# A seven-tap convolution and a gated layer on Trainium2: how the tap weights reach the 128 partitions

## The chip, the core and the metric

The kernel runs on one core of a Trainium2 chip. Five engines with queues of their own work side by side: TensorE (PE: matmuls, and PEld for its weight loads), VectorE (DVE), ScalarE (ACT), GpSimd (POOL) and SyncE (SP). SP, ACT and POOL also issue DMA transfers between the main memory (HBM) and the on-chip memory of 128 partitions. Matmuls write to PSUM, an accumulator of 128 partitions, and VectorE or ScalarE take the results out of it. The engines wait for each other, and for transfers, with semaphores[...].

The metric is device time in microseconds (us), median of several runs. The kernel before took 690.42 us (three runs, 689.95 to 690.78). Profiles are of one run each, and their span leaves out a little at the ends: 688.2 us for the kernel before.

## The reference, cut to what matters

```python
# x: 8 x 4096 x 192, weight: 8 heads x 7 taps, w_in: 192 x 2048, w_out: 2048 x 192, beta: 2048
w = softmax(weight, axis=-1)                 # exp(weight - max) / (sum + 1e-9), per head
x_pad = concat([zeros(8, 6, 192), x], axis=1)
conv[b, s, 24*h + g] = sum over k of w[h, k] * x_pad[b, s + k, 24*h + g]
h = conv.reshape(32768, 192) @ w_in
g = h * sigmoid(beta * h)                    # swish with a beta for each of the 2048 columns
out = g @ w_out
```

Channel 24h+g belongs to head h. Only the seven taps of each head, 56 numbers in all, come from `weight`; before they can be used they must stand in each partition that holds a channel of that head.

## The kernel before

The rows are cut into two streams (NS = 2) that run in the two halves of the partitions. The 192 channels are stored as 64 groups of three (Q = 64, NK = 3), so 64 partitions hold one stream and eight neighbouring partitions share a head. A step is a stretch of rows of both streams; steps 0, 1 and 2 are small (128, 128 and 256 rows), so that the pipeline fills quickly. From step 3 on VectorE computes the convolution. For the first 512 rows TensorE does: the taps, times an identity matrix, are its weights (`diag`), and 14 matmuls per 128 rows add up the seven shifted products of the two streams.

The loads that the start needs. The taps come as two transfers that repeat each head's row for its eight partitions, one for each half, after the first block of x on the same two queues:

```python
taps = consts.tile([128, K], FP32, name="taps")
for s, eng in enumerate((nc.sync, nc.scalar)):
    pin(eng.dma_start(out=x0[:, 0, s, :], in_=xs[s, 0:128, :]))
for s, eng in enumerate((nc.sync, nc.scalar)):
    pin(eng.dma_start(out=taps[half_of(s), :],
                      in_=weight[:, None, :].to_broadcast([H, Q // H, K])))
# ... beta16 and x0 of block 1 follow on nc.sync
# nc.scalar then loads its table for Exp
# GpSimd: ident = affine_select(...), then it issues the loads of w_in (256, 384 and 384
# columns for each half), xb0 (blocks 2 and 3 of x), w_out, ...
```

The softmax numerators, the weights of the convolution, and the first block. `warm` issues matmuls on a constant whose results nobody reads:

```python
warm(9, 256)                                       # 9 matmuls of 256 columns
cv0 = psum_h.tile([128, 2, TILE], FP32, name="ph")
pin(nc.vector.tensor_reduce(out=nmax, in_=taps, axis=AX.X, op=ALU.max, negate=True))
pin(nc.scalar.activation(etap, taps, AF.Exp, bias=nmax, accum_out=tsum))
for k in range(2):
    make_diag(k)                                   # VectorE: diag[k] = ident2 * etap[:, k]
# ...
t = transpose_0(pa[0], x0, 0)                      # TensorE: 3 transposes of 128x128 f32
take_0(t, 0, act=True)                             # ScalarE: xr <- PSUM
warm(6, 128)
for k in range(2, K):
    make_diag(k)
# ...
pin(nc.scalar.activation(scrap, one, AF.Silu))     # brings the table of Silu in early
b0 = [cv0[:, 0, :], pb[0]]
conv_0(b0, 0)                                      # 7 taps x 2 streams = 14 matmuls of 384 columns
evac_0(b0, 0, 0, nc.scalar)
evac_0(b0, 0, 1, nc.vector)                        # xcp, the input of step 0
t1 = transpose_0(pa[1], x0, 1)
pin(nc.tensor.transpose(beta_ps, beta16, ident[0:NF, 0:NF]))
```

Step 0 then runs u = 0 to 7. Each u has six matmuls with `w_in` into one PSUM tile `ph` (of which there are two) and two activations of 128x256 on ScalarE (`gp`); between them TensorE transposes and convolves the next blocks:

```python
def first_tile(i, u):
    if (i, u) == (0, 1):
        take_0(transpose_0(pa[0], xb0, 0), 2)      # needs xb0, block 2
        conv_0(pb, 1, 0, 1)
    elif (i, u) == (0, 2):
        take_0(transpose_0(pa[1], xb0, 1), 3)      # needs xb0, block 3
        conv_0(pb, 1, 1, 2)
    # ... further taps and blocks
```

u = 5 is the first to use the last 384 columns of `w_in`.

Of the kernel before, what the change touches and what calls it, by code (L numbers as in the profile page):

```python
# [10 lines left out]
FP32 = mybir.dt.float32  # L11
FP32R = mybir.dt.float32r
BF16 = mybir.dt.bfloat16
AF = mybir.ActivationFunctionType
ALU = mybir.AluOpType
AX = mybir.AxisListType
# [3 lines left out]
def kernel(  # L20
# [9 lines left out]
    nc = tc.nc  # L30

    B, S, D = x.shape
    H, K = weight.shape
# [5 lines left out]
    Q = D // NK  # L39
    NS = 2  # L40
# [5 lines left out]
    def pin(ins):  # L46

        return tc.keep_in_program_order(ins)
# [4 lines left out]
    consts = ctx.enter_context(tc.tile_pool(name="consts", bufs=1))  # L53
# [55 lines left out]
    def half_of(s):  # L109
        return slice(64 * s, 64 * s + 64)  # L110
# [8 lines left out]
    x0 = consts.tile([128, 2, NS, D], FP32, name="x0")  # L119
    xb0 = consts.tile([128, 2, NS, D], BF16, name="xb0")  # L120
    xb1 = consts.tile([128, 2, NS, D], BF16, name="xb1")
    taps = consts.tile([128, K], FP32, name="taps")
    for s, eng in enumerate((nc.sync, nc.scalar)):
        pin(eng.dma_start(out=x0[:, 0, s, :], in_=xs[s, 0:128, :]))  # L124
    for s, eng in enumerate((nc.sync, nc.scalar)):
        pin(eng.dma_start(out=taps[half_of(s), :],
                          in_=weight[:, None, :].to_broadcast([H, Q // H, K])))
    beta16 = consts.tile([NF, 128], FP32, name="beta16")
    pin(nc.sync.dma_start(out=beta16, in_=moe_beta.rearrange("(c p) -> c p", p=128)))
    HF = F // 2  # L130
# [1 line left out]
    def load_x0(b, eng):  # L132
# [7 lines left out]
    scrap = consts.tile([128, 1], FP32, name="scrap")  # L140
    pin(nc.scalar.activation(scrap, one, AF.Exp))

    ident = consts.tile([128, 128], FP32, name="ident")
    pin(nc.vector.memset(ident, 0.0))
    pin(nc.gpsimd.affine_select(out=ident, in_=ident, compare_op=ALU.not_equal, fill=1.0,
                                base=0, pattern=[[-1, 128]], channel_multiplier=1))
    for f0, f1 in ((0, 256), (256, 640), (640, HF)):
# [7 lines left out]
    for s in range(NS):  # L155
        pin(nc.gpsimd.dma_start(out=xb1[:, :, s, :],
                                in_=xs[s, TILE:TILE + 256, :].rearrange("(b p) d -> p b d", p=128)))
# [21 lines left out]
    def warm(n, cols):  # L179
        for _ in range(n):  # L180
            pin(nc.tensor.matmul(idle[:, 0, 0:cols], ones[:, 0:128], ones[:, 0:cols], start=True, stop=True))

    warm(9, 256)
    cv0 = psum_h.tile([128, 2, TILE], FP32, name="ph")
    nmax = consts.tile([128, 1], FP32, name="nmax")
    pin(nc.vector.tensor_reduce(out=nmax, in_=taps, axis=AX.X, op=ALU.max, negate=True))
    etap = consts.tile([128, K], FP32, name="etap")
    tsum = consts.tile([128, 1], FP32, name="tsum")
    pin(nc.scalar.activation(etap, taps, AF.Exp, bias=nmax, accum_out=tsum))  # L189
    diag = consts.tile([128, K, NS, Q], FP32R, name="diag")  # L190

    def make_diag(k):
# [19 lines left out]
    def take_0(t, b, act=False):  # L212
        dst = xr[:, :, PAD + 128 * b:PAD + 128 * b + 128]
        if act:
            pin(nc.scalar.activation(dst, t, AF.Copy))  # L215
        else:
            pin(nc.vector.tensor_copy(dst, t))
# [20 lines left out]
    pb = po_banks()  # L238
    t = transpose_0(pa[0], x0, 0)
    take_0(t, 0, act=True)  # L240
    warm(6, 128)
    for k in range(2, K):
        make_diag(k)
    rsum = consts.tile([128, 1], FP32, name="rsum")
# [219 lines left out]
    for i in range(NP, n_steps):  # L464
        j = steps[i][0] // TILE + 1
# [140 lines left out]
```

## Time and profile before

| What | Value |
|---|---|
| Time, median of three | 690.42 us |
| Span of the profile | 688.2 us |
| TensorE busy | 681.2 us (99%) |
| ScalarE busy | 586.5 us (85%) |
| VectorE busy | 553.2 us (80%) |
| GpSimd busy | 14.1 us (2%) |
| Share of the chain that ended last: PE, ACT, DMA | 97%, 1%, 1% |

Busy time is an average over the whole span, and TensorE is busy nearly throughout. The page's second part cuts the span into 40 slices of about 17 us; the first slice has a 7 for PE where the others have a 9. The change touches only what lies in the first 8 us, so the views to read are those with a window on the start: the chain of waits (what released what, followed back from the end), the timeline of each engine, and the list of DMA issues with the time from issue to landing. In the chain and the timeline the first column is the start in us, the second the duration of the merged group, and a bracket gives the idle time ahead of it with what ended it. The column PEclk reads full speed in the whole span, so that the pace of TensorE has to be taken from the starts of its matmuls.

### The profile page before, as it was taken

The numbers are of one execution on the slowest core, as the hardware profiler recorded it, in microseconds if no ns is written. First come the engines' busy times: TensorE is split into PE (matmuls) and PEld (weight loads), VectorE is DVE, ScalarE is ACT, GpSimd is POOL, SyncE is SP. The second block draws the span as 40 slices with busy tenths as digits, with TensorE's granted clock in tenths as the row PEclk, the third lists the DMA queues.
The fourth block names the chain that finished last, engine by engine and source line by source line (L and its number), as shares of the span: only waits on it lengthen the run. The fifth ranks groups of instructions, "written<-read, shape, count | busy, mean of one in ns | idle before, by whom it ended". The sixth has DMA issues, their size and how long they took to land.

```text
span 688.2 us, 27039 instructions
## 1 busy us (share of the span) xinstructions
PE 681.2 (99%) x12426; PEld 451.1 (66%) x12426; DVE 553.2 (80%) x902; ACT 586.5 (85%) x600; POOL 14.1 (2%) x25
## 2 busy tenths in 40 slices
PE   7999999999999999999999999999999999999998
PEld 5799986555555555555555555555555567777777
DVE  4999999999998889878889888888888898875112
ACT  5999999888888888888888888888888888888881
POOL 7000000000000000000000000000000000000000
PEclk9999999999999999999999999999999999999999
DMA  9554333354334344323344323444224443220113
GB/s 212 157 139 113 89 105 90 89 134 108 102 76 106 105 118 117 80 62 106 105 117 116 79 63 106 105 117 116 72 70 105 106 117 71 56 55 12 48 49 92
DMA packets 148977, 66.84 MB, mean 97 GB/s; under 512 B 110672, under 2 KB 148256, under 8 KB 148864
## 3 DMA queue, kind: packets, MB, share of 16 engines
q1 hardware_dynamic: 145480, 61.08, 34.5%
q0 software_dynamic: 3168, 3.93, 2.7%
q8 instruction: 97, 1.59, 1.0%
q14 instruction: 16, 0.13, 0.1%
q10 hardware_dynamic: 216, 0.10, 0.0%
HBM read 28.32 MB, written 25.17 MB: 78 GB/s over the span
## 4 chain that ended last, share of the span: by engine, by line
PE 97%; ACT 1%; DMA 1%; DVE 0%; issue 0%; SPq 0%; DVEq 0%
PE ph L330 47%; PE po L408 41%; PE po L362 6%; PE po L446 2%; PE ph L313 1%; ACT gp L317 1%; DMA taps<-in_weight_dram 1%; ACT g L317 1%; PE ph L223 0%; PE po L209 0%; PE po L223 0%; ACT etap L189 0%; SPq L124 0%; ACT xr L215 0%; DVE o_sp L368 0%
## 5 line engine op out<-in xcount | busy, mean ns | idle before, releaser
L334 ACT ACTIVATE g<-ph,beta 128x1024 bf16<-128x1024 f32 (+1 forms) x544 | 560.4, 1038 | 79.0 <-PE ph L330 63.4
L330 PE MATMUL ph<-xc,w_in_s 64*64 64x512 bf16 (+2 forms) x5856 | 589.3, 366 | 0.3 <-ACT g L317 0.3
L408 PE MATMUL po<-g,w_out_q 64*64 64x512 bf16 x5184 | 528.5, 376 | 0.0
L330 PEld LDWEIGHTS <-w_in_s 64*64 64x64 bf16 (+1 forms) x5856 | 271.5, 104 | 126.8 <-issue 0.5
L296 DVE SCALAR_TENSOR_TENSOR acc<-xt,tapn,acc 128x512 f32<-128x512 bf16 (+1 forms) x450 | 311.3, 763 | 0.9
L408 PEld LDWEIGHTS <-w_out_q 64*64 64x64 bf16 x5184 | 240.0, 105 | 91.9
L425 DVE STREAM_TRANSPOSE o_sb<-po 128x512 f32<-128x512 f32 x81 | 72.0, 889 | 110.3 <-PE po L408 110.3
L296 DVE SCALAR_TENSOR_TENSOR xc<-xt,tapn,acc 128x512 bf16<-128x512 bf16 (+1 forms) x90 | 64.1, 763 | 0.1
L362 PE MATMUL po<-w_out_s,g 64*128 64x192 bf16 x896 | 57.1, 243 | 0.0
L86 DVE CAST xb<-xf 128x768 bf16<-128x768 f32 (+1 forms) x62 | 48.7, 824 | 0.0
L362 PEld LDWEIGHTS <-g 64*128 64x128 bf16 x896 | 43.4, 94 | 3.3
L294 DVE TENSOR_SCALAR acc<-xt,tapn 128x512 f32<-128x512 bf16 (+1 forms) x90 | 41.0, 488 | 1.1
L368 DVE COPY o_sp<-po 128x192 f32<-128x192 f32 x40 | 12.7, 350 | 9.7 <-PE po L446 7.3
L313 PE MATMUL ph<-xcp,w_in_s 64*128 64x256 bf16 (+1 forms) x144 | 15.0, 316 | 0.2 <-ACT gp L317 0.2
L317 ACT ACTIVATE gp<-ph,beta 128x256 bf16<-128x256 f32 x32 | 12.4, 479 | 1.8 <-PE ph L313 1.8
L446 PEld LDWEIGHTS <-g 128*128 128x128 bf16 x128 | 10.5, 98 | 0.4 <-issue 0.4
L446 PE MATMUL po<-w_out_s,g 128*128 128x192 bf16 x128 | 10.7, 246 | 0.0
L317 ACT ACTIVATE g<-ph,beta 128x512 bf16<-128x512 f32 x16 | 9.6, 692 | 0.2
L313 PEld LDWEIGHTS <-w_in_s 64*128 64x128 bf16 x144 | 6.8, 97 | 3.6 <-issue 1.0
L223 PE MATMUL po<-xr,diag 64*128 64x384 f32 x49 | 8.9, 401 | 0.0
L362 PE MATMUL po<-w_out_s,gp 64*128 64x192 bf16 x128 | 7.2, 243 | 0.0
L362 PEld LDWEIGHTS <-gp 64*128 64x128 bf16 x128 | 5.8, 94 | 1.6
(49 smaller groups left out, 60.1 us busy)
## 6 DMA issues: line engine op xcount, KB each, us to landing
xf<-in_x_dram SPq DMA_DIRECT2D x60, 384.0 KB, 3.9
out_dram<-o_sb SPq DMA_DIRECT2D x108, 192.0 KB, 4.6
out_dram<-o_sp SPq DMA_DIRECT2D x16, 192.0 KB, 4.1
xt<-xb SPq DMA_TRANSPOSE x122, 3.0
w_out_f<-in_moe_w_out_dram POOLq DMA_DIRECT2D x4, 384.0 KB, 7.3
w_in_s<-w_in_s POOLq DMA_DIRECT2D x4, 192.0 KB, 6.0
out_dram<-o_sp SPq DMA_DIRECT2D x8, 96.0 KB, 1.6
w_in_s<-in_moe_w_in_dram POOLq DMA_DIRECT2D x4, 144.0 KB, 4.9
```

The lines of the kernel that those rows point to most:

```text
L86: pin((eng or nc.vector).tensor_copy(xbf_of[j][:, b0:b1, :, s, :].rearrange("p b k q -> p k b q"), xf_of[j][:, b0:b1, s, :].rearrange("p b ...
L294: pin(nc.vector.tensor_scalar_mul(a, src, w))
L296: pin(nc.vector.scalar_tensor_tensor(out=xc_of[i][:, k0:k1, 0:n] if k == K - 1 else a, in0=src, scalar=w, in1=a, op0=ALU.mult, op1=ALU.add))
L313: pin(nc.tensor.matmul(ph[:, h, 0:NS * n], w_in_s[half_of(h), kk, ts(fcs[h], 128)], xc_of[i][half_of(h), :, kk, :], start=(kk == 0), stop= ...
L317: pin(nc.scalar.activation(g_at(i, fcs[h])[:, :, 0:n], ph[:, h, 0:NS * n].rearrange("p (s t) -> p s t", s=NS), AF.Silu, scale=beta[:, fcs[ ...
L330: pin(nc.tensor.matmul(ph[m0:m1, s, 0:n], w_in_s[half_of(s), kk, 128 * fc + m0:128 * fc + m1], xc_of[i][half_of(s), kk, 0:n], start=(kk == ...
L334: pin(nc.scalar.activation(g_at(i, fc)[:, :, 0:n], ph[:, :, 0:n], AF.Silu, scale=beta[:, fc:fc + 1]))
L362: pin(nc.tensor.matmul(po[q][:, 0:D], g_at(i, fc)[r, s, ts(b, 128)], w_out_s[r, fc, :], start=(phase == 0 and fc == 0), stop=(phase == 1 a ...
L368: pin(nc.vector.tensor_copy(dst, po[:, 0:D]))
L408: pin(nc.tensor.matmul(po_of[i, m][half_of(s), 0:n], w_out_q[half_of(r), fc, m, :], g_at(i, fc)[half_of(r), s, 0:n], start=(first and fc = ...
L425: pin(nc.vector.transpose(osb_of[i][:, 0:n // L, :, m], po_of[i, m][:, 0:n].rearrange("p (b l) -> p b l", l=L)))
L446: pin(nc.tensor.matmul(po[:, 0:D], g_at(i, fc)[:, s, ts(b, 128)], w_out_s[:, fc, :], start=(fc == 0), stop=(fc == NF - 1)))
```

## The change

The taps are loaded once, as a tile of 8 heads by 7 taps (224 bytes), by the first transfer on SyncE's queue; SyncE's half of the first block of x follows it. A matmul spreads them: its weights are a selection matrix `sel` of 8 x 128 with a one where partition and head belong together, so its result, in an unused bank of `cv0`, holds each head's taps in each of its partitions. VectorE and ScalarE read the taps from there. VectorE clears `sel`, and GpSimd fills it ahead of `ident`. Three short filler matmuls stand between that matmul and the transposes of x, and the fillers after the transposes are seven instead of six: they give TensorE work while it would wait. The two repeating loads of the taps are gone from both queues.

```diff
-    taps = consts.tile([128, K], FP32, name="taps")
+    taps = consts.tile([H, K], FP32, name="taps")
+    pin(nc.sync.dma_start(out=taps, in_=weight))
     for s, eng in enumerate((nc.sync, nc.scalar)):
         pin(eng.dma_start(out=x0[:, 0, s, :], in_=xs[s, 0:128, :]))
-    for s, eng in enumerate((nc.sync, nc.scalar)):
-        pin(eng.dma_start(out=taps[half_of(s), :],
-                          in_=weight[:, None, :].to_broadcast([H, Q // H, K])))
...
+    sel = consts.tile([H, NS, H, Q // H], FP32, name="sel")
+    pin(nc.vector.memset(sel, 0.0))
     ident = consts.tile([128, 128], FP32, name="ident")
     pin(nc.vector.memset(ident, 0.0))
+    pin(nc.gpsimd.affine_select(out=sel, in_=sel, compare_op=ALU.not_equal, fill=1.0, base=0,
+                                pattern=[[0, NS], [-1, H], [0, Q // H]], channel_multiplier=1))
     pin(nc.gpsimd.affine_select(out=ident, in_=ident, compare_op=ALU.not_equal, fill=1.0,
                                 base=0, pattern=[[-1, 128]], channel_multiplier=1))
...
     warm(9, 256)
     cv0 = psum_h.tile([128, 2, TILE], FP32, name="ph")
     nmax = consts.tile([128, 1], FP32, name="nmax")
-    pin(nc.vector.tensor_reduce(out=nmax, in_=taps, axis=AX.X, op=ALU.max, negate=True))
+    tap_ps = cv0[:, 1, 0:K]
+    pin(nc.tensor.matmul(tap_ps, sel.rearrange("h s g j -> h (s g j)"), taps, start=True, stop=True))
+    warm(3, 128)
+    pin(nc.vector.tensor_reduce(out=nmax, in_=tap_ps, axis=AX.X, op=ALU.max, negate=True))
...
-    pin(nc.scalar.activation(etap, taps, AF.Exp, bias=nmax, accum_out=tsum))
+    pin(nc.scalar.activation(etap, tap_ps, AF.Exp, bias=nmax, accum_out=tsum))
...
     take_0(t, 0, act=True)
-    warm(6, 128)
+    warm(7, 128)
```

## The prediction

> **What bounds the kernel now.** I read the page's table of busy time first: TensorE 99% of the span. From about 34 us on the chain of waits is TensorE alone, and the change adds or removes nothing there. What it can move is the moment at which that stretch begins, so I read the start. First view: the chain of waits, window 0 to 25 us (start, duration, what).
>
> ```profile
> 0.74 0.39 SPq L124
> ...
> 1.19 4.75 DMA taps<-in_weight_dram
> ...
> 6.04 0.17 DVE nmax L186
> ...
> 6.23 0.39 ACT etap L189 x2
> 6.63 0.39 ACT xr L215
> ...
> 7.09 0.66 PE ph L223
> ```
>
> For 4.75 us the path is the load of the taps. The first block of x is not on it: its copy out of PSUM (`xr`) merely queues behind `etap` on ScalarE. The timeline of TensorE shows the same from the other side:
>
> ```profile
> 0.78 2.08 PE L181 MATMUL ph<-const-bfloat16-1.0 128*128 128x256 bf16 x9 [0.78 <-PEq L590]
> 3.44 0.88 PE L209 MATMUL po<-ident,x 128*128 128x128 f32 x3 [0.58 <-DMA x<-in_x_dram]
> 4.11 0.84 PE L181 MATMUL ph<-const-bfloat16-1.0 128*128 128x128 bf16 x6
> 7.09 0.66 PE L223 MATMUL ph<-xr,diag 64*128 64x384 f32 x1 [2.14 <-ACT xr L215]
> ...
> 8.19 0.52 PE L223 MATMUL ph<-xr,diag 64*128 64x384 f32 x1
> ...
> 8.51 0.52 PE L223 MATMUL ph<-xr,diag 64*128 64x384 f32 x1
> ```
>
> x was there at 3.44, the convolution began at 7.09, with 2.14 us of idle TensorE before it. Its pairs start 0.32 us apart (8.19, 8.51): 384 columns in 0.32 us are 1.2 columns per ns. In the timeline at 13.76 six such matmuls, three pairs, take 0.77 us with the drain, about 0.2 a pair. So the first convolution runs slow. What follows it is led by ScalarE:
>
> ```profile
> 11.54 2.34 ACT L317 ACTIVATE gp<-ph,beta 128x256 bf16<-128x256 f32 x6 [1.26 <-PE ph L313]
> 14.05 6.32 ACT L317 ACTIVATE gp<-ph,beta 128x256 bf16<-128x256 f32 x16 [0.16 <-PE ph L313]
> ```
>
> Once the first `gp` starts, ScalarE hardly pauses (0.16 us up to 20.4). So the start of the first `gp`, 11.54, is the mark to follow. What it gains reaches the end, unless a load is missing.
>
> Last view, the DMA issues up to 20 us (size, then median us from issue to landing):
>
> ```profile
> x<-in_x_dram SPq DMA_DIRECT2D x1, 192.0 KB, 4.5
> x<-in_x_dram ACTq DMA_DIRECT2D x1, 96.0 KB, 2.6
> x<-in_x_dram SPq DMA_DIRECT2D x1, 96.0 KB, 2.4
> ```
>
> The first block of x takes 2.4 to 2.6 us when nothing is ahead of it.
>
> [...] The trace agrees with the two paces (1.2 columns per ns above; 256 columns of L313 at 0.21 us a pair near 10.7, about 0.12 near 12.5), and the change to the fast one came near 11.5, 4.4 us after 7.09. [...]
>
> **The change part by part.**
>
> *Taps.* Issued at 0.74. I take 2.0 to 2.2 us to landing, my estimate, a little under the 2.4 of the 96 KB load in the table above: it lands near 2.85. TensorE's nine fillers hand over near 2.75 (the pace of 0.21 us each from 0.78), so the spreading matmul waits hardly at all. It is of the kind of the beta transpose (f32, 16 columns, 0.28 us with its drain in the timeline), so its result stands near 3.15. `sel` is ready at about 1.3.
>
> *The softmax numerators.* `nmax` 0.16 and `etap` 0.39 from the rows above, with 0.05 between: about 3.8. ScalarE is free for it: without its taps issue (1.20 us in its timeline) the table load of 1.28 us ends near 2.5. The seven `diag` take 1.71 us in VectorE's timeline, 0.245 each: from 3.9 to 5.6, the first at 4.1. They have left the path.
>
> *x.* SyncE's half is issued after the taps: 0.74 + 0.39 + 0.06 = 1.19, plus 2.4 is 3.59, where ScalarE's half landed at 3.34 and TensorE started 0.10 later. So the transposes move from 3.44 to 3.7, a loss of 0.25. From their start to the convolution: 0.88 for the transposes, 0.03, then `xr` 0.39 and 0.08 as in the chain, which is 1.4. The convolution starts at 5.1 instead of 7.09, a gain of 2.0. The fillers fit: 0.67 (hand-over of the transposes, 4.11 less 3.44) and 7 x 0.107 us is 1.42, so they end just as it starts and cost nothing.
>
> *The clock.* If TensorE is still slow at 5.1, all that follows keeps its durations: the mark goes to 9.5, gain 2.0. If the nearly unbroken work from 0.78 has released the clock by then (4.4 us after 0.78 is 5.2), the convolution's seven pairs take about 0.21 instead of 0.32 each, 0.8 us less; the transposes and the beta transpose after it (1.05 us in the chain) lose 0.4, of which the copy out of the first convolution (0.58) leaves perhaps 0.3; and the first six matmuls with `w_in` lose 0.3. That is 1.4 more, 3.4 in all, a mark near 8.1.
>
> *What was added.* GpSimd's second select costs 0.29, partly where it waited: its first load is issued 0.2 later (1.62 for 1.42). VectorE's memset is under 0.1 and beside other work. Four more fillers and one matmul lie in idle time.
>
> **The loads as the next wait.** From issue and landing: the first 256 columns of `w_in` land at 6.4, xb0 at 8.9 and 9.4, the last `w_in` piece at 12.1; add 0.2. TensorE takes xb0's first block 0.4 after the mark (11.94 less 11.54). At a mark of 9.5 that is 9.9, no wait. At 8.1 it is 8.5 against 9.1: 0.6 us lost, perhaps 0.5 at ScalarE. u = 5 took its columns at 15.07; 3.4 earlier is 11.7, plus the 0.5 already lost 12.2, against 12.3: nothing much. So the fast-clock case yields about 2.9.
>
> **Sum.** Slow clock 2.0, fast clock 2.9; I give them nearly equal weight[...]. 2.4 us off 690.42 is 688.0.
>
> **The rivals.** (1) *The small load does not land early, or holds up x.* Then x takes the place of the taps as the bound. For it: `beta`, also small, took 4.1 us to land; against it, that one was queued behind the repeating loads. Every tenth that x is late is a tenth lost; with 1 us the gain is about 1, a time of 689.4. (2) *The clock stays slow*: the fillers leave two gaps, at the taps and before x[...]: 688.4. (3) *The early DMA queue is the next bound*: GpSimd's loads do not move forward, so a faster start meets xb0 and `w_in`. It caps the gain near 3, 687.4, and may take a little of it in the first case too. (4) *Nothing reaches the end*, because VectorE's convolution for step 3 or its inputs set the pace: against it, from 34 us on TensorE is never idle for long and waits for VectorE 0.2 us in all between 80 and 660 us. That would be 690.4.
>
> **Range and chances.** The cases lie between 687.4 and 689.4, and the runs of the kernel before are themselves 0.8 us apart. I take 686.9 to 689.5. Two per cent would be 13.8 us; the whole stretch before the convolution is 7.1 us, so faster by over 2% is as good as excluded. Slower by over 2% would need a disturbed steady stretch, which the change does not touch: 0.005 each, 0.99 for within.
>
> **What would show it right or wrong.** In the changed profile: the wait for the taps is gone from the chain and the load of x is in its place; the transposes start near 3.7; the first convolution near 5.1, its pairs 0.32 or 0.21 apart, which tells the clock; `gp` first at 9.5 or 8.1; an idle stretch of TensorE or ScalarE released by xb0 if the loads bind; the stretch from 34 us as long as before. I am wrong if the transposes start after 4.2, if a wait for the taps remains, or if the first `gp` moves and the end does not.

## The result and the profile after

The changed kernel takes 687.3 us (four runs, 686.99 to 688.03), beside 690.6 us (four runs, 689.95 to 690.98) for the kernel before. The ratio is 0.9955, with a 95% interval of 0.9937 to 0.9972: 3.3 us faster, within 1.9 to 4.4. That lies in the stated range, and most of the foretold mechanism shows in the profile. The size depends on the times of the kernel before: in two later comparisons the same pair differs by 1.2 and 1.4 us. The span of the changed kernel's profile is 685.3 us, 2.9 less than before.

The chain of waits of the changed kernel, window 0 to 26 us (start, duration, what):

```profile
1.10 0.40 POOL sel L146
1.50 0.25 POOL ident L148
1.75 2.57 POOL w_in_s L113 x4
4.32 4.64 DMA xb<-in_x_dram
...
21.00 1.43 PE ph L319 x12
```

The taps have left the path, and the first block of x has not taken their place. Now the chain runs through GpSimd: it fills `sel` and `ident`, issues four loads of `w_in`, and then issues xb0 block 2, which lands at 8.96. (It issues xb0 ahead of the last piece of `w_in`, not behind it as the comment in the code above lists them.) The last line is the start of step 2. In the chain of the kernel before it stood later:

```profile
23.92 1.43 PE ph L313 x12
```

The timeline of TensorE in the changed kernel:

```profile
2.79 0.59 PE L190 MATMUL ph<-taps,sel 8*128 8x7 f32 x2
3.31 0.50 PE L184 MATMUL ph<-const-bfloat16-1.0 128*128 128x128 bf16 x3
3.61 0.80 PE L215 MATMUL po<-ident,x 128*128 128x128 f32 x3
4.24 0.57 PE L184 MATMUL ph<-const-bfloat16-1.0 128*128 128x128 bf16 x7
4.99 0.44 PE L229 MATMUL ph<-xr,diag 64*128 64x384 f32 x1 [0.17 <-ACT xr L221]
...
5.62 0.34 PE L229 MATMUL ph<-xr,diag 64*128 64x384 f32 x1
...
5.79 0.33 PE L229 MATMUL ph<-xr,diag 64*128 64x384 f32 x1
...
9.00 0.35 PE L215 MATMUL po<-ident_b,xb 128*128 128x128 bf16 x3 [0.85 <-DMA xb<-in_x_dram]
```

No bracket for a wait stands at the taps matmul, so its load was there in time. The seven fillers at 4.24 take 0.57 us together; before, at the slow pace, six took 0.84. TensorE thus turned from its slow pace to its fast one near 4.2 (one of the expectations below says 3.9), and the pairs of the convolution start 0.18 us apart (5.62, 5.79) instead of 0.32. Then TensorE idles 0.85 us, until xb0 lands. The prediction and the expectations call this turn the release of the clock. The profiles show the two paces but no clock behind them: in the kernel before, PEclk reads 1.00 both from 7.09 to 9.60 us, with pairs 0.32 apart, and from 11.50 to 14.90, where they are about 0.2 apart. ScalarE, whose first `gp` was the mark to follow:

```profile
7.87 1.57 ACT L323 ACTIVATE gp<-ph,beta 128x256 bf16<-128x256 f32 x4 [0.76 <-DVE xr L223]
10.11 0.84 ACT L323 ACTIVATE gp<-ph,beta 128x256 bf16<-128x256 f32 x2 [0.67 <-PE ph L319]
```

The mark moved from 11.54 to 7.87, that is by 3.67. Most of the difference to the 2.92 that step 2 gains is lost in the pause of 0.67 ahead of 10.11. The DMA issues up to 20 us (size, median us from issue to landing):

```profile
x<-in_x_dram SPq DMA_DIRECT2D x1, 192.0 KB, 3.8
x<-in_x_dram ACTq DMA_DIRECT2D x1, 96.0 KB, 2.0
x<-in_x_dram SPq DMA_DIRECT2D x1, 96.0 KB, 1.9
```

Each of these lands sooner after its issue than before (4.5, 2.6 and 2.4), without the repeating loads on the same queues.

From the start of step 2 to the end the profiles take the same time: span less start of step 2 is 664.3 before (688.2 less 23.92) and 664.3 after (685.3 less 21.00), and between 664.2 and 664.5 in every profile below. So the start of step 2 is the whole difference between these profiles, and a profile can be compared to a tenth of a us although the times scatter by more.

### The profile page after: what moved, and what is told of

Read it like the earlier page. It is cut to its first block, busy times and chain, and to the rows that moved or that the text cites. A ratio compares the mean times of both kernels' runs of the same rounds, so it can differ in the third digit from the quotient of the medians.

```text
span 685.3 us, 27052 instructions
## 1 busy us (share of the span) xinstructions
PE 679.9 (99%) x12432; PEld 450.4 (66%) x12432; DVE 553.2 (81%) x903; ACT 587.1 (86%) x600; POOL 14.5 (2%) x26
## 4 chain that ended last, share of the span: by engine, by line
PE 97%; ACT 1%; DMA 1%; POOL 0%; issue 0%; DVE 0%; POOLq 0%
PE ph L336 47%; PE po L414 41%; PE po L368 6%; PE po L452 2%; PE ph L319 1%; ACT gp L323 1%; DMA xb<-in_x_dram 1%; ACT g L323 1%; POOL w_in_s L113 0%; PE po L229 0%; PE po L215 0%; POOL sel L146 0%; DVE o_sp L374 0%; POOL ident L148 0%; POOLq L146 0%
## 5 line engine op out<-in xcount | busy, mean ns | idle before, releaser
L336 PE MATMUL ph<-xc,w_in_s 64*64 64x512 bf16 (+2 forms) x5856 | 560.2, 366 | 0.3 <-ACT g L323 0.3
L414 PE MATMUL po<-g,w_out_q 64*64 64x512 bf16 x5184 | 499.3, 376 | 0.0
L336 PEld LDWEIGHTS <-w_in_s 64*64 64x64 bf16 (+1 forms) x5856 | 263.5, 104 | 121.4 <-issue 0.5
L414 PEld LDWEIGHTS <-w_out_q 64*64 64x64 bf16 x5184 | 231.3, 106 | 97.3
```

Of the source, the lines that this page charges most:

```text
L336: pin(nc.tensor.matmul(ph[m0:m1, s, 0:n], w_in_s[half_of(s), kk, 128 * fc + m0:128 * fc + m1], xc_of[i][half_of(s), kk, 0:n], start=(kk == ...
L414: pin(nc.tensor.matmul(po_of[i, m][half_of(s), 0:n], w_out_q[half_of(r), fc, m, :], g_at(i, fc)[half_of(r), s, 0:n], start=(first and fc = ...
```

## The experiments

They were timed in three series, e1 to e4, e5 to e8 and e9 to e12, each on another chip (0, 9 and 13) and each beside the kernel before, which had medians of 688.7, 688.7 and 688.9 us there and ran from 687.1 to 692.1. Ratios to it have their 95% interval in brackets. Where a theory "expected 21.0", the first profile of the changed kernel is meant.

| Run | Median us, ratio | Convolution starts | Fast pace from about | Step 2 starts |
|---|---|---|---|---|
| e1, no fillers | 687.81, 0.9989 [0.9976, 1.0002] | 4.80 | 13.9 | 23.54 |
| e2, four fillers fewer | 687.46, 0.9980 [0.9971, 0.9990] | 4.80 | 6.4 | 20.84 |
| e3, before with fillers | 688.00, 0.9983 [0.9975, 0.9992] | 7.08 | 7.0 | 22.30 |
| e4, xb0 early | 688.34, 0.9993 [0.9983, 1.0003] | 5.13 | 6.2 | 22.51 |
| e5, before again | 688.58, 0.9993 [0.9982, 1.0005] | 6.27 | 11.7 | 23.44 |
| e6, after again | 687.57, 0.9980 [0.9968, 0.9992] | 5.11 | 5.1 | 21.31 |
| e7, xb0 late | 690.46, 1.0019 [1.0008, 1.0029] | 5.13 | 9 | 23.04 |
| e8, loads first | 688.07, 0.9985 [0.9977, 0.9994] | 5.52 | 6.9 | 22.99 |
| e9, block 2 by SyncE | 687.12, 0.9967 [0.9953, 0.9981] | 5.13 | 6.7 | 21.23 |
| e10, the same, no fillers | 688.02, 0.9983 [0.9975, 0.9990] | 4.80 | 9 | 21.64 |
| e11, taps second | 688.31, 0.9989 [0.9981, 0.9997] | 5.84 | 8.9 | 22.16 |
| e12, after, third | 687.50, 0.9980 [0.9973, 0.9987] | 5.13 | 8.7 | 22.09 |

The moment of the turn to the fast pace is read from the matmuls of one profile each: where pairs of 384 columns turn from 0.32 us apart to 0.18, or the other matmuls by the same proportion.

**The kernel before and the changed one again (e5, e6, e12; no edit).**

> The kernel before once more, unchanged, for a second profile of it. If what varies in its time is the landing of the repeating taps load and the moment at which the clock is released, the profile shows a convolution starting somewhere between 5.6 and 7.1 and pairs of 0.32 us that turn to 0.18 at some point, and step 2 begins earlier than 23.92 by the sum of the two. If the kernel before always starts as in its first profile, the convolution starts at 7.1 with slow pairs, step 2 at 23.9.

Its chain of waits:

```profile
1.20 3.83 DMA taps<-in_weight_dram
```

The same two small loads took 3.83 us here and 4.75 in the first profile. The convolution followed at 6.27 instead of 7.09, that is 0.82 sooner. The pace was slow until 11.7, and step 2 began only 0.48 sooner (23.44). So the first theory holds in part: the landing of the taps varies, and the first profile caught a late one. It is not shown to make up the whole variation of the times. This run took 689.5 us and is one of the six longest of its 22; no run near the median of 688.6 was profiled. By the constant rest of 664.3, step 2 would begin near 22.5 in such a run, an estimate.

> The changed kernel once more, unchanged, for a second profile. Theory, xb0 caps the start: even if the clock is released later than in the first profile (near 3.9), the convolution starts at 5.0, and step 2 at 21.0 within 0.3, time within 0.5 of 687.3. If the release of the clock decided its time, step 2 and the time would move by up to 1 us with it.

> The changed kernel unchanged, as the measure for the three beside it. As in its two profiles: convolution at 5.0 to 5.1, a wait for xb0 of 0.85 to 1.0, step 2 at 21.0 to 21.3, 687.3 to 687.6 us.

In e6 the fast pace came near 5.1, and all went as expected. In e12 it came later. TensorE in e12:

```profile
4.24 0.95 PE L184 MATMUL ph<-const-bfloat16-1.0 128*128 128x128 bf16 x7
...
6.57 0.52 PE L229 MATMUL ph<-xr,diag 64*128 64x384 f32 x1
...
6.89 0.52 PE L229 MATMUL ph<-xr,diag 64*128 64x384 f32 x1
...
8.72 0.85 PE L319 MATMUL ph<-xcp,w_in_s 64*128 64x256 bf16 x12
...
9.51 0.35 PE L215 MATMUL po<-ident_b,xb 128*128 128x128 bf16 x3
```

The pairs are 0.32 apart to the end of the convolution. The block of twelve at 8.72 is fast (0.85 us; 1.46 at the slow pace in e1), so the turn came near 8.7. TensorE then needs xb0 only at 9.51, and there is no wait. The first `gp` starts at 9.29, which is 1.4 later than in the first profile, and step 2 at 22.09, 1.1 later. Not all of that is due to the late turn. The chain of waits of e12 goes through another load, blocks 4 and 5 of x (tile `xb1`), which GpSimd issues behind `w_out`:

```profile
10.73 9.64 DMA xb<-in_x_dram
...
20.50 0.49 PE po L215 x6
```

This load took 9.64 us, where it took 7.6 to 8.1 in the other two profiles. TensorE stood idle for 0.44 us until it landed, and its transposes began 0.94 after the matmuls ahead of them instead of 0.44. So about 0.5 of the 1.1 us belong to this load, and about 0.6 are left for the late turn: more than the first theory of e6 allows, less than the 1 us of the other. The profiled run is also the second longest of its 22 (688.27). The fillers do not ensure an early turn (4.2, 5.1 and 8.7 in three profiles of one kernel).

**The fillers, taken away (e1, e2) and alone (e3).**

```diff
 e1                     e2                        e3 (on the kernel before)
-    warm(3, 128)      -    warm(3, 128)         -    warm(6, 128)
-    warm(7, 128)      -    warm(7, 128)         +    warm(30, 128)
                       +    warm(6, 128)
```

> The changed kernel without the three fillers ahead of the transposes and without the seven after them (the nine at the start stay). Theory, the clock of TensorE counts and the fillers release it: the convolution still starts near 5.0, but its pairs start 0.32 us apart instead of 0.18, the first gp starts near 9.3 instead of 7.87, the wait for xb is gone, and step 2 begins near 21.9 instead of 21.00; 0.9 us longer than the changed kernel. Rival, the early taps do it all and the fillers are stuffing: pairs 0.18, first gp 7.9, step 2 at 21.0, same time as the changed kernel.

TensorE in e1:

```profile
3.33 0.89 PE L214 MATMUL po<-ident,x 128*128 128x128 f32 x3
4.80 0.68 PE L228 MATMUL ph<-xr,diag 64*128 64x384 f32 x1 [0.58 <-ACT xr L220]
...
6.25 0.52 PE L228 MATMUL ph<-xr,diag 64*128 64x384 f32 x1
...
6.57 0.52 PE L228 MATMUL ph<-xr,diag 64*128 64x384 f32 x1
```

Pairs of 0.32 and a first `gp` at 9.26, as the theory said. The pace stayed slow until about 13.9, and step 2 began at 23.54. But this profile belongs to the three longest of its 14 runs (689.7 to 689.9); the others took 687.5 to 688.1. The median is 0.2 to 0.3 above the changed kernel's in the later series and 0.35 above e2's in the same one, not 0.9. The fillers are therefore no mere stuffing. That they pay in some executions only, those with a late turn, fits these times, but only one of the long runs was profiled. Without them the convolution starts 0.2 to 0.3 earlier (4.80 for 4.99 to 5.13).

> The changed kernel with the fillers of the kernel before: none ahead of the transposes, six after them. If the four added fillers are what releases the clock: pairs 0.32, first gp near 9.3, step 2 near 21.9. If it is the disappearance of the idle stretch of 2.14 us, and the gap of about 0.4 us ahead of the transposes does not matter: pairs 0.18, first gp near 7.9, step 2 at 21.0, same time as the changed kernel. I hold the second for likelier.

In its profile the fast pace came in the middle of the convolution, near 6.4, the first `gp` at 8.47, and yet step 2 at 20.84, no later than with all fillers, because xb0, which TensorE needed next, came only at 8.8. Its ratio is that of the changed kernel. The four added fillers bring nothing that can be measured; the early taps with the six old fillers bring it all. A fast pace from 6.4 on thus cost nothing in this profile, while one from 8.7 on in e12 cost about 0.6.

> The kernel before with 30 instead of six fillers after the first transposes, nothing else; its taps still land near 5.9. Theory, the clock is a part of the gain of its own: the fillers go from 0.107 to about 0.06 us each and end near 6.1, the convolution still starts at 7.1, its pairs 0.18 apart, first gp near 10.0 instead of 11.54, no wait for xb, step 2 near 22.4 instead of 23.92; 1.5 us shorter than the kernel before. Rival, fillers gain nothing by themselves: first gp at 11.5 or, if the clock stays slow and the fillers run to 7.3, at 11.8; same time as the kernel before.

TensorE in e3:

```profile
4.02 3.13 PE L181 MATMUL ph<-const-bfloat16-1.0 128*128 128x128 bf16 x30
7.08 0.44 PE L223 MATMUL ph<-xr,diag 64*128 64x384 f32 x1
...
7.55 0.34 PE L223 MATMUL ph<-xr,diag 64*128 64x384 f32 x1
...
7.72 0.34 PE L223 MATMUL ph<-xr,diag 64*128 64x384 f32 x1
```

In the profile the size was right (step 2 at 22.30, 22.4 expected), and the reason half so; the median is only 0.7 below that of the kernel before, not 1.5. The taps landed near 4.5 in this run, and the copy `xr` ended at 5.57; the fillers, at the slow pace almost to their end (3.13 us for 30), themselves held the convolution until 7.08. With its pairs 0.18 apart it still gave a first `gp` at 9.97 and step 2 at 22.30, sooner than in e5, whose convolution started 0.8 earlier with slow pairs. Over 22 runs the ratio is 0.9983: the earlier fast pace is worth something by itself. The spread is small (687.4 to 688.6), perhaps because fillers up to 7.1 cover later taps as well. The fillers alone thus gain 0.7 us and the early taps with the six old fillers (e2) 1.3, while the changed kernel with both gains 1.2 to 1.4: the two parts overlap and do not add up.

**The load that caps the start (e4, e7, e8, e9).**

```diff
 e4: after each of the first two pieces of w_in one block of xb0
-        if f0 == 256:
-            for b in range(2, NB):
-                load_x0(b, nc.gpsimd)
+        if n + 2 < NB:                      # n = 0, 1, 2 for the pieces
+            load_x0(n + 2, nc.gpsimd)
 e7: -        if f0 == 256:      +        if f0 == 640:
 e8: e4, and the two affine_select moved behind the first piece of w_in
 e9: x0 holds blocks 0 to 2 in f32, xb0 block 3 alone
     load_x0(1, nc.sync)
+    load_x0(2, nc.sync)
-            for b in range(2, NB):
-                load_x0(b, nc.gpsimd)
+            load_x0(3, nc.gpsimd)
```

> The changed kernel with the two xb0 loads issued after the last piece of w_in, 1.24 us later. If xb0 caps the start, block 2 lands near 10.2 instead of 8.96, TensorE waits for it about 2 us instead of 0.85, step 2 begins near 22.2 and the kernel is 1.2 us longer than the changed one. If ScalarE's own work or w_in were the cap, at most 0.4 us would be lost.

TensorE in e7:

```profile
11.05 0.35 PE L215 MATMUL po<-ident_b,xb 128*128 128x128 bf16 x3 [1.18 <-DMA xb<-in_x_dram]
```

The block was issued at 5.59 and took 5.42 us: it landed at 11.0, 1.8 to 2.0 after its landing in the changed kernel (8.96 and 9.23). The wait stands although the fast pace came late here (near 9). The median is 2.9 above e6's, but that is not the cap alone: in the twelve longest runs (690.35 to 693.01) the granted clock over the whole run was 0.995 to 0.998, for which no run here shows a cause, while all runs of e6 have 1.0. The ten runs of e7 at 1.0 took 688.96 to 689.69, median 689.2, which is 1.6 above e6's; 1.2 was expected. So the load does cap the start, and the 0.4 beyond that fit its longer landing (5.42 us instead of 4.64 and 4.91).

> The changed kernel, GpSimd's loads in another order: xb0 block 2 after the first piece of w_in, block 3 after the second. Theory, xb0 caps the gain at the start: block 2 lands near 7.6 instead of 8.96, TensorE no longer waits 0.85 us for it; the second piece of w_in lands 0.7 later, near 9.4, and takes part of that back at u = 2; step 2 begins 0.2 to 0.8 us earlier than 21.00. Rival, xb0 was only the last of several equal waits: step 2 stays at 21.0.

TensorE in e4:

```profile
8.74 0.35 PE L214 MATMUL po<-ident_b,xb 128*128 128x128 bf16 x3
...
10.29 0.50 PE L318 MATMUL ph<-xcp,w_in_s 64*128 64x256 bf16 x5 [0.62 <-DMA w_in_s<-in_moe_w_in_dram]
```

The wait for xb0 is gone, but `w_in` takes its place, and its last piece lands only at 13.64, 7.24 after its issue. Step 2 begins at 22.51; the median is 0.8 above e6's and 0.9 above e2's in the same series. (Five of its 22 runs have a granted clock of 0.997; the median of the others, 688.07, is still 0.6 above e2's.) The theory failed: in this order what xb0 gained was lost with `w_in` behind it.

> The changed kernel, GpSimd issuing the first piece of w_in ahead of its two selects (it waits for VectorE there anyway), then the selects, xb0 block 2, the second piece, block 3, the last piece. From the changed kernel's rows: sel ready near 2.5, ident near 2.8, so the taps matmul at 2.8 and the transposes at 3.6 are not held up; all later loads go out about 0.4 us earlier than in the order with xb0 early. Theory, the start is held by what the DMA queue has delivered: step 2 near 21.0 to 21.5, better than the order with xb0 early (22.5) and not clearly better than the changed kernel. Rival, the order is what counts: step 2 near 20.3.

TensorE in e8:

```profile
3.18 0.59 PE L190 MATMUL ph<-taps,sel 8*128 8x7 f32 x2 [0.33 <-POOL sel L150]
...
12.01 0.35 PE L215 MATMUL po<-ident_b,xb 128*128 128x128 bf16 x3 [1.55 <-DMA xb<-in_x_dram]
```

Two misses: `sel` was ready only at 3.13, which held up the taps, and block 3 came 6.66 us after its issue. The new order is not better than the changed kernel. Why the late loads take 6.7 to 7.2 us in these two orders, and the same loads 4.3 to 6.4 in the first profile, in e2 and in e12, stays open.

> The changed kernel with block 2 of x loaded uncast by SyncE, after block 1, and transposed in f32; GpSimd loads block 3 alone. Theory, block 2 on GpSimd's queue is the cap: it now lands near 6.5 and the wait of 0.85 to 0.99 us is gone; block 3 goes out where block 2 did and lands near 9.1, just when it is needed; f32 transposes cost 0.26 more. Step 2 begins near 20.4 instead of 21.0 to 21.3, and the kernel is 0.6 to 0.9 us shorter than the changed one. Rival, all early transfers share one rate and whatever lands last takes the place of block 2: no gain over the changed kernel, a wait for block 3 or w_in in its place.

TensorE in e9:

```profile
8.21 0.83 PE L319 MATMUL ph<-xcp,w_in_s 64*128 64x256 bf16 x12
8.97 0.61 PE L215 MATMUL po<-ident,x 128*128 128x128 f32 x3
```

The block by SyncE's queue was there in time: no bracket, no wait. The fast pace came near 6.7 in this profile, and it shows no gain: step 2 at 21.23, where e2, with block 2 on GpSimd's queue and the fast pace from 6.4, began it at 20.84. The runs speak for one in part: three of seven took 686.4 to 686.6, less than any run of the changed kernel (686.99 at best). The ratio, 0.9967, is lower than e12's 0.9980 in the same batch, but the intervals overlap; a gain over the changed kernel of about 0.4 us is possible, not settled.

> The kernel with block 2 by SyncE, without the three and the seven fillers. Theory, once the cap is off, the moment at which the clock is released counts in full: 1 us or more longer than with the fillers, and a wider spread. Rival, the loads still cap the start: same as with the fillers within 0.4.

The edit is e9 without `warm(3, 128)` and `warm(7, 128)`. The median is 0.9 above e9's, near the 1 us of the theory, and the runs spread from 686.4 to 688.6. In the profile the fast pace comes near 9, after the whole convolution, and step 2 begins 0.4 later than in e9's. That fits the theory that with the cap off the moment of the turn counts in full. But two runs reached 686.4 without the fillers too, and no run that short was profiled, so it is not shown.

**The order of the two loads (e11).**

```diff
-    pin(nc.sync.dma_start(out=taps, in_=weight))
     for s, eng in enumerate((nc.sync, nc.scalar)):
         pin(eng.dma_start(out=x0[:, 0, s, :], in_=xs[s, 0:128, :]))
+    pin(nc.sync.dma_start(out=taps, in_=weight))
```

> The changed kernel with the load of the taps behind SyncE's half of x instead of ahead of it. x lands 0.4 earlier, the taps 0.45 later, near 3.2; TensorE waits 0.4 for them ahead of the spreading matmul, so the transposes start near 4.0 and the convolution near 5.4 instead of 5.1. Theory, xb0 caps the start: step 2 begins at 21.0 to 21.3 all the same, the time is that of the changed kernel within 0.2. Rival, the order of the two loads counts: 0.3 to 0.5 longer.

TensorE in e11:

```profile
3.52 0.56 PE L190 MATMUL ph<-taps,sel 8*128 8x7 f32 x2 [0.67 <-DMA taps<-in_weight_dram]
```

My theory fell. The load took 2.20 us from its issue at 1.19, the convolution came at 5.84, and the median is 0.8 longer than e12's in the same batch; its fastest run is 0.6 behind e12's fastest. The cap should have hidden such a delay when the fast pace comes early; in this profile the pace was slow until about 8.9. Whether the gap of 0.67 us in TensorE's work also delays the turn is a guess that no run tested. That the taps go ahead of x is worth 0.8 us.

## Why the prediction was right

The predicted path held in most of its steps.

- *Taps off the path.* Foretold: landing near 2.85, hardly a wait. The matmul began at 2.79 without one. Rival 1 fell. What makes the repeating loads slow no run here separates.
- *Softmax.* `etap` was foretold to end near 3.8 and `diag` to begin at 3.9. ScalarE was done with it at 3.97 and VectorE began at 4.01; the convolution did not wait for either. The 0.2 come from the spreading matmul: it stands twice in the timeline (x2) and took 0.59 us there, where I had taken 0.28.
- *x.* Here a term was wrong. I took 2.4 us from issue to landing and so a start at 3.7; x took 1.9 and landed near 3.1. What set 3.61 was TensorE's own queue: the taps matmul and three fillers, without which the transposes began at 3.33 in e1. So the load of x did not take the place of the taps in the chain, as I had said it would. That the sum came out the same is luck: two errors cancelled.
- *Convolution.* Foretold 5.1, measured 4.99, 5.11 and 5.13.
- *Clock.* Foretold as two cases of nearly equal weight (my estimate), first `gp` at 9.5 or 8.1. Three profiles show 7.87, 8.00 and 9.29. Both cases exist, and rival 2 with them; that its two gaps delay the turn was not shown. My moment for the turn, 4.4 us after the first matmul at 0.78, was an estimate from the single turn in the profile of the kernel before (near 11.5, 4.4 us after 7.09). It is no rule: the turn came 3.4, 4.3 and 7.9 us after that matmul.
- *The cap.* Foretold 0.6 us of waiting for xb0 in the fast case, 0.85 and 0.99 measured, and none in the slow case, as in e12. A load that I had not counted, `xb1`, took about 0.5 there. The fast case was to yield 2.9, and the span fell by 2.9. Rival 3 held.
- *The end.* Rival 4 fell: the rest stayed at 664.3.

The mis-sized term is the one that I read as fixed: the start of the kernel before. Its repeating load took 4.75 us in the first profile, 3.83 in e5 and landed earlier still in e3, and its times vary by 5 us. With it the gain varies: 3.3 us in the first comparison, where the kernel before ran at 690.6; 1.2 us (688.73 less 687.57) and 1.4 us (688.90 less 687.50) in the later ones. My 2.4 lies between, as the mean of two cases for the pace taken from one early profile; that it fits so well is partly luck. The different landing of the taps alone does not explain the two sizes. All four runs of the kernel before in the first comparison took 689.95 us or more, and only 28 of the 191 timed beside the experiments did. Whether the chip plays a part was not tested, and why the first four were long stays open.

What the change does in all these series is to narrow the times: the 42 runs of the changed kernel lie between 687.0 and 688.3 but for one at 690.1 (granted clock 0.997), the 22 of e5 between 687.2 and 692.0. Four of those 22 took 687.2 to 687.5, no longer than the changed kernel usually does.

## What to carry to other kernels

A wait on a tiny load at the start was cheap to remove here: load the few numbers once, first on the queue, and let an idle TensorE spread them. Then ask what each later stage needs next, with issue and landing from the trace: here a load that had not moved forward took back a fifth of what the mark had gained (0.75 of 3.67 us), and in the two other orders that were tried on its queue another load was late. And before a duration from one profile goes into a sum, look at it in a second profile: a load that varies by 1 us (4.75 and 3.83 here), or a turn to the fast pace that varies by 4 (4.2 to 8.7), matters when the gain is 2.

## What the hardware showed beside this

- TensorE turned to its fast pace at 4.2, 5.1 and 8.7 us in three runs of one kernel with nearly unbroken work from 0.78 on, and at about 13.9 in one run without the fillers around the transposes.
- f32 transposes change their pace too: three take 0.91 us in e12 at 7.67, while slow, and 0.61 at 6.43 in the changed kernel.
- Behind the repeating loads (1.8 KB on each queue) the 8 KB load of `beta` took 4.1, 2.7 and 3.3 us to land (first profile, e3, e5); in the three profiles of the changed kernel, without them, 1.8, 1.7 and 1.9. It took 3.0 in e8, where GpSimd's loads go out sooner, so they are not its only delay.
- GpSimd's select on 8 x 128 elements took 0.40 us, the one on 128 x 128 right after it 0.28.
